# Moving short waits in TensorE's order: the decay check's transpose, the logits of blocks 1 to 3, the last second product, the steps beside row copies, and busy matmuls in the first block

## Chip, cores, metric

One core of one Trainium2 chip. The metric is device time of one execution in microseconds (us); the number quoted is the median of several executions, with lowest and highest where they matter. "Span" is the profiled time from the first to the last instruction, some 1.7 us shorter than the device time of the same execution. "Clock" is the mean clock granted to TensorE, 1.00 at full rate.

## The reference, cut to what matters

```python
def _attn_ref(q, k, v, f_logit):          # (4, 8, 768, 48), fp32
    f = 1.0 / (1.0 + np.exp(-f_logit))
    for t in range(S):
        state = f[:, :, t, :, None] * state + np.einsum('bhd,bhe->bhde', k[:, :, t], v[:, :, t])
        y[:, :, t] = np.einsum('bhd,bhde->bhe', q[:, :, t], state)

def _moe_ref(x, w_in, w_out):             # (3072, 384), (384, 2048), (2048, 384)
    h = x @ w_in
    sp = np.maximum(h, 0.0) + np.log1p(np.exp(-np.abs(h)))
    return (h * erf(sp)) @ w_out
```

Attention with a decaying state feeds a product to 2048 hidden columns, an activation, and a product back to 384 columns. All is fp32.

## The kernel before: the parts that matter here

The sequence is cut into 24 chunks of 128 rows; three chunks make a block, and there are 8 blocks. TensorE's order is written by hand. Iteration `it` has one slot per matmul of the hidden product of block `it` (48 slots, 12 per group) and, from `it` 2 on, of the second product of block `it - 2` (48 slots, between the hidden groups); from `it` 2 to 7, where both run, an iteration is called a mixed stage. The profile counts two passes for each of these matmuls (x96 for the 48 slots of a second product). VectorE's or ScalarE's copy of a finished hidden product out of PSUM is called its eviction. Between slots stand pieces of the attention of block `it + 1`, steps of the activation (`act_step`) and steps that round weights.

```python
def prepare(blk, j0, j1):                 # logits of a block: VectorE, then ScalarE twice
    ...
    nc.vector.tensor_scalar(out=lt, in0=lt, scalar1=LOGIT_MIN, scalar2=None, op0=ALU.max)
    ...
    nc.scalar.activation(out=lt, in_=lt, func=AF.Exp, scale=-1.0)
    nc.scalar.activation(out=lt, in_=lt, func=AF.Ln, bias=1.0)

def stage_d(g):                           # decay sums of chunk g
    ...
    nc.tensor.matmul(ps, lhsT=tri[:], rhs=lts[blk][:, j, :], start=True, stop=True)
    nc.scalar.activation(out=dp..., in_=ps..., func=AF.Exp, scale=-1.0)
    nc.scalar.activation(out=kd, in_=ps..., func=AF.Exp)
    nc.vector.tensor_tensor(out=qd..., in0=qns[...]..., in1=dp..., op=ALU.mult)
    ...
# stage_t(g): transposes of qd and kd, copied to SBUF as qT and kT by ScalarE
# stage_s(g): scores; VectorE makes A = scores * tri; state product dS; VectorE makes Sn
# stage_y(g): y = products of A with v and of the state with qT; copied to xT by ScalarE

def project(blk):                         # second product
    ops = [ps_moe.tile([P, 2, 512], FP32, name="ops", tag="moe") for _ in range(2)]
    ...                                   # row copies: osb2 <- ops[0], osb1 <- ops[1], on ScalarE

def check_decays():
    nc.vector.tensor_reduce(out=low[:], in_=Tall..., axis=AX.X, op=ALU.min)
    ps = ps_at.tile([P, 512], FP32, name="ps_f", tag="at")
    nc.tensor.transpose(ps[0:1, 0:P], low[:], ident[:])
    ...                                   # VectorE: minimum of the row, flag

def keep_busy(n):                         # matmuls whose result nobody reads
    ps = ps_sc.tile([P, 2, HP, P], FP32, name="busy", tag="sc")
    for _ in range(n):
        nc.tensor.matmul(ps[:, 0, 0, :], lhsT=tri[:], rhs=tri[:], start=True, stop=True)

for it in range(n_blocks + 2):            # cut
    for s, _ in enumerate(slots(it)):
        ...
        if step:
            act_step()
        if it + 2 < n_blocks and s == n // 2:
            prepare(it + 2, 0, CPB)
        if it == n_blocks - 1 and s == 5:
            check_decays()
```

## Time and profile before

| | before |
|---|---|
| time, median of 3 | 657.68 us (657.57 to 657.77) |
| profiled execution | 656.5 us, span 654.8 us |
| TensorE busy | 632.7 us, 97% of the span |
| mean clock | 0.990 |

The prediction shows the lines that carry the argument. Four more are fixed points of TensorE's order, from the timeline of the kernel before (start, duration, engine, line, operation, output and inputs, and in brackets the idle time before it with its releaser).

```profile
31.17 2.85 PE L480 MATMUL hps<-xT,w_in_sb 128*128 128x384 f32 x8 [0.64 <-ACT xT L421]
...
65.91 1.45 PE L480 MATMUL hps<-xT,w_in_sb 128*128 128x384 f32 x4
...
148.40 3.81 PE L480 MATMUL hps<-xT,w_in_sb 128*128 128x384 f32 x11 [0.33 <-DVE Hg L492]
...
198.99 1.56 PE L480 MATMUL hps<-xT,w_in_sb 128*128 128x384 f32 x4 [1.08 <-ACT osb L521]
```

These four are the first hidden product, the product after the first sum of block 2, the point where TensorE waits for VectorE's eviction, and the pause behind the second row copy of the first mixed stage.

### The profile page before, as it was taken

How to read it: one execution, taken by the hardware profiler on the slowest of the kernel's cores; microseconds unless marked ns; L12 is line 12 of the kernel's file. 1: busy time of each engine (PE TensorE's matmuls, PEld its weight loads, DVE VectorE, ACT ScalarE, POOL GpSimd, SP SyncE). 2: the span in 40 equal slices, each digit the busy share in tenths (PEclk: the TensorE clock that was granted, in tenths of full speed). 3: DMA queues.
4: the chain of work that ended last, by engine and by line, in shares of the span. 5: the costliest groups of instructions: out<-in, count | busy, mean ns of one | idle time of the engine just before them, and what ended most of it. 6: DMA issues, size and time to landing. Idle time of an engine off the chain costs nothing.

```text
span 654.8 us, 9308 instructions
## 1 busy us (share of the span) xinstructions
PE 632.7 (97%) x3785; PEld 393.2 (60%) x3785; DVE 475.7 (73%) x440; ACT 509.9 (78%) x459; POOL 69.2 (11%) x61
## 2 busy tenths in 40 slices
PE   8889998999999999999999999999999989999996
PEld 6756655665655666656666666666666555555553
DVE  4889897997778966778667877688676667587710
ACT  5355655679899988996897978997797969899800
POOL 0112101120110001301310002202020000000000
PEclk9899999999999999999999999999999989999999
DMA  9996952310104120221204201120000000000001
GB/s 195 252 264 156 295 120 37 74 25 14 37 25 85 25 37 13 61 49 25 37 13 98 36 13 24 38 49 1 2 0 37 1 0 1 36 0 2 36 2 40
DMA packets 120689, 36.90 MB, mean 56 GB/s; under 512 B 112448, under 2 KB 115520, under 8 KB 120640
## 3 DMA queue, kind: packets, MB, share of 16 engines
q1 hardware_dynamic: 118560, 35.84, 23.6%
q10 hardware_dynamic: 2080, 0.39, 0.4%
q8 instruction: 32, 0.52, 0.3%
q14 instruction: 17, 0.14, 0.1%
HBM read 31.46 MB, written 4.72 MB: 55 GB/s over the span
## 4 chain that ended last, share of the span: by engine, by line
PE 72%; ACT 12%; DVE 10%; issue 4%; POOL 0%; DMA 0%; SPq 0%; DVEq 0%; POOLq 0%; ACTq 0%
PE ops L509 30%; PE hps L480 29%; ACT x L153 5%; PE y L147 5%; DVE e L158 3%; PE sc L366 3%; PE ps_d L323 2%; PE ps_t L350 2%; ACT L446 1%; ACT yl L435 1%; ACT L297 1%; ACT e L446 1%; PE dS L394 1%; ACT e L431 1%; DVE w_out_sb L272 1%
## 5 line engine op out<-in xcount | busy, mean ns | idle before, releaser
L480 PE MATMUL hps<-xT,w_in_sb 128*128 128x384 f32 x768 | 262.7, 493 | 2.4 <-ACT osb L521 1.1
L509 PE MATMUL ops<-w_out_sb,Hg 128*128 128x384 f32 x768 | 256.1, 489 | 1.5 <-ACT osb L516 1.5
L158 DVE SCALAR_TENSOR_TENSOR e<-x,e 128x1536 f32<-128x1536 f32 x128 | 230.0, 1797 | 5.1
L153 ACT ACTIVATE x<-yl,serf_bias 128x1536 f32<-128x1536 f32 x128 | 195.3, 1566 | 15.2 <-DVE e L158 15.1
L509 PEld LDWEIGHTS ops<-w_out_sb,Hg 128*128 128x128 f32 x768 | 143.8, 190 | 99.7 <-ACT osb L516 2.1
L480 PEld LDWEIGHTS hps<-xT,w_in_sb 128*128 128x128 f32 x768 | 143.7, 192 | 99.7 <-issue 5.3
L449 DVE TENSOR_TENSOR Hg<-Hg,e 128x1536 f32<-128x1536 f32 x32 | 56.2, 1757 | 64.5 <-ACT e L446 64.4
L340 POOL TENSOR_TENSOR kd<-kn,kd 128x384 f32<-128x384 f32 x21 | 34.7, 1652 | 325.5 <-issue 186.3
L492 DVE COPY Hg<-hps 128x768 f32<-128x768 f32 x48 | 45.8, 954 | 20.4 <-PE hps L480 20.0
L446 ACT ACTIVATE e<-e 128x1536 f32<-128x1536 f32 x32 | 47.5, 1483 | 9.8 <-DVE e L158 9.6
L435 ACT ACTIVATE yl<-e 128x1536 f32<-128x1536 f32 x32 | 47.5, 1484 | 0.3
L431 ACT ACTIVATE e<-Hg 128x1536 f32<-128x1536 f32 x32 | 47.2, 1476 | 0.0
L336 DVE TENSOR_TENSOR qd<-qn,dp 128x384 f32<-128x384 f32 x24 | 15.8, 658 | 37.1 <-ACT dp L326 37.1
L410 POOL TENSOR_TENSOR Mbd<-Sn,Tall 48x192 f32<-48x192 f32 x32 | 33.3, 1041 | 88.1 <-DVE Sn L407 71.4
L297 ACT ACT_TABLE_LOAD x31 | 39.8, 1283 | 1.3 <-PEq L915 0.8
L446 ACT ACT_TABLE_LOAD x31 | 39.8, 1283 | 0.6
L147 PE MATMUL y<-A,vt 128*32 128x128 f32 x768 | 36.5, 283 | 1.0 <-DVE A L380 1.0
L147 PEld LDWEIGHTS y<-A,vt 128*32 128x32 f32 x768 | 28.1, 111 | 13.2 <-issue 6.1
L380 DVE TENSOR_TENSOR A<-sc,tri 128x1024 f32<-128x1024 f32 x24 | 29.3, 1220 | 8.5 <-PE sc L366 8.1
L147 PE MATMUL y<-qT,Mbd 128*32 128x128 f32 x480 | 31.2, 280 | 0.0
L366 PEld LDWEIGHTS sc<-qT,kT 48*128 48x128 f32 x384 | 23.3, 187 | 12.5 <-issue 10.6
L421 ACT COPY xT<-y 128x384 f32<-128x384 f32 x24 | 11.3, 472 | 24.0 <-PE y L147 24.0
(70 smaller groups left out, 384.9 us busy)
## 6 DMA issues: line engine op xcount, KB each, us to landing
lt<-in_f_logit_dram SPq DMA_DIRECT2D x24, 192.0 KB, 4.1
qn<-in_q_dram SPq DMA_DIRECT2D x24, 192.0 KB, 3.3
Hg<-in_moe_w_out_dram SPq DMA_DIRECT2D x6, 768.0 KB, 5.5
kn<-in_k_dram SPq DMA_DIRECT2D x23, 192.0 KB, 3.3
vt<-in_v_dram SPq DMA_DIRECT2D x23, 192.0 KB, 3.1
w_out_sb<-in_moe_w_in_dram SPq DMA_DIRECT2D x4, 768.0 KB, 6.4
Hg<-in_moe_w_in_dram SPq DMA_DIRECT2D x4, 768.0 KB, 7.8
out_dram<-osb SPq DMA_DIRECT2D x8, 384.0 KB, 2.5
```

The costliest lines, as they stand in the source:

```text
L147: nc.tensor.matmul(y[M * i : M * (i + 1), kt, :], lhsT=terms[n][0], rhs=terms[n][1], start=(n == 0), stop=(n == len(terms) - 1), skip_grou ...
L153: nc.scalar.activation(out=dst[:], in_=y[:], func=AF.Square, bias=serf_bias[:, i : i + 1], scale=SERF_K)
L158: nc.vector.scalar_tensor_tensor(out=e[:], in0=x[:], scalar=SERF_AB[i][1], in1=e[:], op0=ALU.add, op1=ALU.mult)
L297: nc.scalar.add_instruction(mybir.InstLoadActFuncSet(act_func_set_id=EXP_LN, name=nc.get_next_instruction_name(), engine=mybir.EngineType. ...
L366: nc.tensor.matmul(sc[:, r, a, :], lhsT=kT[rows(r), a, :], rhs=qT[rows(r), a, :], start=True, stop=True,)
L431: nc.scalar.activation(out=e[:], in_=h, func=AF.Exp)
L435: nc.scalar.activation(out=y[:], in_=e[:], func=AF.Ln, scale=SERF_C, bias=1.0)
L446: nc.scalar.activation(out=e[:], in_=e[:], func=AF.Tanh)
L449: nc.vector.tensor_tensor(out=h, in0=h, in1=e[:], op=ALU.mult)
L480: nc.tensor.matmul(hps[:, j, 0:TB], lhsT=w_in_sb[:, kt, ft * P : (ft + 1) * P], rhs=xTs[blk][:, kt, :], start=(kt == 0), stop=(kt == n_k - 1),
L492: nc.vector.tensor_copy(out=to, in_=hps[:, :, 0:TB])
L509: nc.tensor.matmul(ops[tt // 2][:, tt % 2, 0:d_model], lhsT=gr["h"][:, j, tt * P : (tt + 1) * P], rhs=w_out_sb[:, ft, :], start=(ft == 0), ...
```

## The change

The intent is to take pauses away from TensorE without adding useful work: issue what TensorE will wait for earlier (logits), or put the waiting instruction later (the check's transpose); keep ScalarE free where it has to copy rows; give the last product a PSUM tile that nobody has to empty; and cover the pauses of the first block with more matmuls that nobody reads, so that the clock stays up.

```diff
+    busy = []
+    def keep_busy(n):
+        for _ in range(n):
+            nc.tensor.matmul(busy[-1], lhsT=tri[:], rhs=tri[:], start=True, stop=True)
 # stage_d, block 0: the tile of the decay sums
+            busy.append(both[:, 1, P : 2 * P])
 # stage_t, after the transposes of qd
+            if 0 < g < CPB and src is qd:
+                keep_busy(3)
 # stage_y, before y
+        if blk == 0:
+            keep_busy(3)
 # project
-        ops = [ps_moe.tile(...) for _ in range(2)]
+        ops = [ps_moe.tile(...) for _ in range(2 if blk < n_blocks - 1 else 1)]
+        if blk == n_blocks - 1:
+            ops.insert(0, ps_sc.tile([P, 2, 512], FP32, name="ops", tag="sc"))
 # check_decays: a generator in two parts
         nc.vector.tensor_reduce(out=low[:], ..., op=ALU.min)
+        yield
         nc.tensor.transpose(ps[0:1, 0:P], low[:], ident[:])
         ...
+        yield
 # ahead of the first block
+        first = ps_sc.tile([P, 2, HP, P], FP32, name="busy", tag="sc")
+        busy.append(first[:, 0, 0, :])
 # first block
         stage_y(1)
+        prepare(1, 0, CPB)
         ...
         stage_y(2)
         ...
-        prepare(1, 0, CPB)
 # the loop over slots
-                if step:
+                if step and not 66 <= s < 72:
                     act_step()
-                if it + 2 < n_blocks and s == n // 2:
+                if it + 2 < n_blocks and s == (16 if it < 2 else n // 2):
                     prepare(it + 2, 0, CPB)
-                if it == n_blocks - 1 and s == 5:
-                    check_decays()
+                if it == n_blocks - 1 and s in (5, 40):
+                    next(check)
```

The old `keep_busy`, which wrote to a tile of its own, is removed. Its two calls at the start stay, but the second of them (behind the first sum) now writes to the tile of the decay sums as well. The skipped steps are two in the first mixed stage (slots 67 and 70) and one in each later one.

## The prediction

> **What bounds the kernel now.** I began with the page: busy time by engine, and the row of the granted clock.
>
> ```profile
> PE 632.7 (97%) x3785; PEld 393.2 (60%) x3785; DVE 475.7 (73%) x440; ACT 509.9 (78%) x459; POOL 69.2 (11%) x61
> ...
> PEclk9899999999999999999999999999999989999999
> ```
>
> TensorE has work in 97% of the span, so only three things shorten it: fewer matmuls, fewer pauses of TensorE, or fewer matmuls at a low clock. No useful matmul is removed, so I look for pauses and for low clock (the two 8s in the clock row). Next, the list of waits, for PE alone; columns are total us, times, longest.
>
> ```profile
> PE ps_d L323 <- ACT lt L312: 3.9, 4, 2.0
> PE ps_f L546 <- DVE low L542: 2.9, 1, 2.9
> PE ps_t L350 <- ACT qT L354: 1.7, 2, 1.0
> PE ops L509 <- ACT osb L516: 1.5, 1, 1.5
> ...
> PE hps L480 <- ACT osb L521: 1.1, 1, 1.1
> ...
> PE y L147 <- DVE A L380: 1.0, 1, 1.0
> ```
>
> All PE waits of that list sum to some 16 us; the diff names nearly every line of it. Then stretches of 4 us; after PE, PEld, DVE, ACT and POOL busy comes the granted clock, the third number from the right. Of all such stretches before the tail, only these have a clock under 1.00.
>
> ```profile
> 24.00:28.00 4.00, 3.02 (x56) 2.79 (x55) 2.92 (x7) 0.34 (x1) 0.48 (x1) 0.87 0.86 165
> 28.00:32.00 4.00, 3.36 (x51) 2.65 (x44) 3.90 (x5) 1.30 (x2) 1.12 (x2) 0.70 1.02 269
> 112.00:116.00 4.00, 3.67 (x6) 2.06 (x7) 1.47 (x3) 3.05 (x5) 0.98 (x1) 0.57 0.01 0
> 524.00:528.00 4.00, 2.27 (x5) 1.36 (x6) 2.10 (x4) 3.31 (x3) 0.00 (x0) 0.66 0.00 0
> 528.00:532.00 4.00, 4.00 (x13) 2.37 (x12) 0.62 (x1) 3.43 (x3) 0.00 (x0) 0.91 0.00 0
> ```
>
> So a pause is paid twice where it lets the clock fall. The timeline shows the pauses one by one (start, duration, and in brackets the idle time and its releaser):
>
> ```profile
> 112.33 1.65 PE L323 MATMUL ps_d<-lt,tri 128*128 128x384 f32 x2 [2.04 <-ACT lt L312]
> 114.53 0.56 DVE L336 TENSOR_TENSOR qd<-qn,dp 128x384 f32<-128x384 f32 x1 [3.19 <-ACT dp L326]
> ...
> 525.73 0.37 PE L546 MATMUL ps_f<-ident,low 128*1 128x128 f32 x1 [2.88 <-DVE low L542]
> ...
> 617.95 31.23 PE L509 MATMUL ops<-w_out_sb,Hg 128*128 128x384 f32 x96 [1.47 <-ACT osb L516]
> ...
> 623.41 1.76 DVE L449 TENSOR_TENSOR Hg<-Hg,e 128x1536 f32<-128x1536 f32 x1 [1.55 <-ACT e L446]
> ```
>
> TensorE stands still at 110.3 for the logits of block 3, at 522.9 for the decay check's minimum, and at 616.5 for a copy of output rows that frees PSUM.
>
> **What the Trainium skill says.** (1) "TensorE: Matmul & The Clock Gate", Part 1: the array's clock has two states, half and full; activity is watched in free-running windows of about 3.4 us, and an idle window brings half rate. The trace agrees on the two states (0.50 in each us from 27 to 30), but not that only an idle window does it: pauses of 0.98, 2.04 and 2.88 us were enough here, in stretches with many short matmuls. (2) The same page, Part 2, step 1: TensorE alone reorders, and only weight loads; matmuls keep program order, and the other engines' queues are in order. The trace agrees: all later matmuls stood 2.88 us behind one 128x128 transpose. So moving an instruction in the order can be worth its whole wait. (3) "PSUM — Partial Sum Buffer", Specifications: 8 banks per partition. The kernel's pools take them all (2 scores, 2 attention, 4 second stage), so another buffer for the last product must be borrowed. (4) "ScalarE: Activation LUTs", What ACT_TABLE_LOAD costs: some 1283 ns per load; the trace's mean is 1283 ns.
>
> **The change part by part.**
>
> *Decay check.* The minimum stays where it was; its transpose comes 35 slots of TensorE later. In the order as built it has no semaphore left to wait for. Removed: 2.88 us, and the low clock after it: four weight loads at 526.54, 527.18, 527.82 and 528.46 are 0.64 us apart where 0.32 is usual, 4 x 0.32 = 1.3. VectorE, which empties the PSUM tile, is idle 4.78 us there, so it takes no part of this. **-4.2 us.**
>
> *Logits of block 3* (the prepare of slot 24 moved to slot 16; eight slots at some 0.65 us, with attention work between them, put it over 5 us earlier). Removed: 2.04 us and the low clock: 1.65 instead of some 0.9 for the sum, 3.07 instead of 2.1 for six passes, together 1.7. So 3.7 us of TensorE. But VectorE works almost without a pause from 114.5 to 159.5, and TensorE waits for it again at 148.4 (0.33 us, for an eviction). VectorE gains only its own pause, 3.19 less some 0.3. The rest becomes a longer wait at 148.4. **-2.9 us.** *Blocks 1 and 2*: the same wait is 0.71 us at 34.73 and 0.48 at 65.16. **-1.2 us.**
>
> *No activation steps where rows are copied.* In the first mixed stage the two row copies stood at 192.07 and 198.48, with squares between; TensorE paused 0.39 and 1.08 us. As built they now stand side by side. ScalarE is full there, so the first pause stays. **-1.1 us.** In later stages such copies cost TensorE nothing.
>
> *Last second product in the scores' PSUM.* It starts without the copy at 617.12. **-1.5 us.**
>
> *Busy matmuls.* Six groups of three are new, 18 x 2 passes x some 0.116 us (from 12 passes in 1.50 at full clock) = 0.7 us per group. Three lie in pauses of 1.01, 0.68 and 0.98 us and cost nothing; two lie where TensorE did not pause (before the y of chunks 0 and 1), one in the pause before y of chunk 2 with part of the pause left. And a dependency is new: they write to the tile of the decay sums, and as built the first group after each sum waits for ScalarE's second exponential of that tile. For chunk 0 the exponential ends at 7.95, where busy matmuls ran from 6.88: later copies queue behind other ScalarE work anyway, so of 1.1 us about 0.2 remain. For chunk 2 it ends at 17.47, where y began at 16.50: with 0.7 of busy work y begins 1.9 later. By the chunk-1 y the delay is 2.5; then the pauses of 0.98 us and behind A take up part, and y of chunk 2 begins at some 29.7 instead of 27.33. If the clock stays full it takes 1.7 instead of 3.2, and the first hidden product starts 0.9 later than 31.17; if it still falls, 2.0 later. I take the middle: **+1.4 us.**
>
> *What is given back in the tail.* Skipping one step in each mixed stage puts the activation work further behind. Counting the steps slot by slot, and in the built order, one whole group more remains behind the row copies of block 5: 12.83 us of ScalarE (distance of its table loads, 568.31 to 581.58 to 594.41 to 607.24). Before, the last tanh ended 55.9 us after the copy at 567.50; now 55.9 + 12.8 + 1.8 (it waits for the second copy) = 70.5, and the product on VectorE ends at 72.3. TensorE needs it after 112 slots of 0.645 us = 72.3. A tie: **+0.3 us.**
>
> Sum: -4.2 - 2.9 - 1.2 - 1.1 - 1.5 + 1.4 + 0.3 = -9.2, so 657.7 - 9.2 = **648.5 us**, 1.4% less.
>
> **Rivals.** (A) *The new waits at the start weigh more*: the busy groups stall TensorE at every exponential and the clock falls all the same, because a busy group is short against the window. For it: the waits are in the built order, and before the change 0.98 us of pause was enough. Against: after 31 us weight rounding has over 4 us in hand. Time: 650 to 651. (B) *ScalarE becomes the bound of the tail*: the tie above falls on the wrong side by a step or two, or VectorE takes all of the gain at 148.4. For it: ScalarE is full from 568 to 620. Time: 651 to 653. (C) *Nothing is given back*: the start costs nothing and the clock stays full throughout; -4.2 -3.7 -1.2 -1.5 -1.5 and -1.4 from the start: 644 to 645. Against: VectorE's full stretch. (D) *The pause at 522.9 was hidden*, so its removal only moves it. Against: TensorE runs from there to 616 with no pause over 0.3 us.
>
> **Range and chances.** The two large terms (4.2 and 2.9) rest on pauses that the trace shows directly; the start may be off by 1.5, the tail by 2, the VectorE stretch by 1. Together about 3 either way, a little more upward: 645 to 652. Two per cent faster needs 644.5, the best of (C): 0.06. Slower by 2% has no mechanism: 0.01. Within 2%: 0.93.
>
> **What would show it.** Right: no PE wait for `ps_f`; none of 0.4 us or more for the logits; PE clock 1.00 around 112 and 524; a longer PE wait for VectorE's eviction near 145; the last product following the one before it with no pause, and ScalarE's last tanh within 2 us of the slot that needs it. The first hidden product starts at 32 to 33. Wrong: a first hidden product before 31 or after 34; a clock under 1.00 in the first 35 us together with a start later than 33; a pause over 2 us inside the last product; or a new pause in the stages from 200 to 500, where I expect none.

## The result, and the profile after

| | before | after |
|---|---|---|
| time, median of 4 each | 657.62 us (656.17 to 657.77) | 648.09 us (648.01 to 648.13) |
| profiled span | 654.8 us | 646.4 us |
| TensorE busy | 632.7 us | 630.7 us |
| mean clock | 0.990 | 0.998 |

The ratio is 0.986, with a 95% interval of 0.984 to 0.988. A ratio here is the mean time of one kernel's fast runs over that of the other's in the same rounds, so it is not quite the ratio of the medians quoted.

First the page of the kernel after: TensorE's busy time and the row of the clock, in which the two 8s are gone.

```profile
PE 630.7 (98%) x3815; PEld 393.8 (61%) x3815; DVE 474.6 (73%) x440; ACT 510.0 (79%) x459; POOL 59.1 (9%) x61
...
PEclk9999999999999999999999999999999999999999
```

Then the list of TensorE's waits of the kernel after (total us, times, longest):

```profile
PE ps_t L357 <- DVE Sn L416: 2.5, 2, 1.6
PE ps_d L320 <- ACT kd L336: 1.9, 2, 1.0
...
PE ops L524 <- DVE Hg L460: 1.2, 1, 1.2
...
PE hps L491 <- ACT osb L531: 0.4, 1, 0.4
```

The waits for `low`, for the logits `lt` and for the copy ahead of the last product are no longer in it. Of the lines shown, the first is new and was not predicted, the second was, and the third only as a tie. Most of the stretches that had a low clock before, of the kernel after (columns as in the prediction; the clock is the third number from the right):

```profile
28.00:32.00 4.00, 3.46 (x82) 2.96 (x81) 3.53 (x6) 1.44 (x2) 1.61 (x2) 1.00 0.99 239
...
112.00:116.00 4.00, 4.00 (x40) 2.66 (x39) 3.86 (x4) 2.55 (x4) 1.81 (x1) 1.00 0.08 4
...
524.00:528.00 4.00, 4.00 (x14) 2.41 (x13) 4.00 (x4) 4.00 (x4) 0.00 (x0) 1.00 0.00 0
528.00:532.00 4.00, 4.00 (x14) 2.33 (x13) 3.08 (x4) 3.98 (x3) 0.00 (x0) 1.00 0.00 0
```

All are at 1.00, and 24 to 28 is too. Last, the timeline of TensorE of the kernel after, at the fixed points and at the new waits:

```profile
7.76 1.60 PE L320 MATMUL ps_d<-tri 128*128 128x128 f32 x12 [0.96 <-ACT kd L336]
...
17.45 0.94 PE L320 MATMUL ps_d<-tri 128*128 128x128 f32 x6 [0.96 <-ACT kd L336]
...
32.19 2.85 PE L491 MATMUL hps<-xT,w_in_sb 128*128 128x384 f32 x8 [0.61 <-ACT xT L432]
...
37.36 0.63 PE L357 MATMUL ps_t<-ident,qd 128*128 128x128 f32 x4 [0.40 <-DVE qd L343]
...
60.26 0.63 PE L357 MATMUL ps_t<-ident,kd 128*128 128x128 f32 x4 [1.59 <-DVE Sn L416]
...
66.48 1.45 PE L491 MATMUL hps<-xT,w_in_sb 128*128 128x384 f32 x4
...
118.57 0.63 PE L357 MATMUL ps_t<-ident,kd 128*128 128x128 f32 x4 [0.90 <-DVE Sn L416]
...
146.01 4.14 PE L491 MATMUL hps<-xT,w_in_sb 128*128 128x384 f32 x12 [0.33 <-DVE Hg L503]
...
577.31 54.34 PE L524 MATMUL ops<-w_out_sb,Hg 128*128 128x384 f32 x168
632.90 8.01 PE L524 MATMUL ops<-w_out_sb,Hg 128*128 128x384 f32 x24 [1.25 <-DVE Hg L460]
```

The difference of the two kernels at each fixed point is a ledger. Each row's change is the difference at this point less that at the row above. The last column is the same change with the second profile of the kernel before (`before_again`, below) in the place of the first.

| up to | before, us | after, us | change in the row | predicted | against `before_again` |
|---|---|---|---|---|---|
| first hidden product | 31.17 | 32.19 | +1.0 | +1.4 | +1.8 |
| product behind the transposes of block 1's first chunk | 39.03 | 38.62 | -1.4 | -0.7 | -2.9 |
| product behind the first sum of block 2 | 65.91 | 66.48 | +1.0 | -0.5 | +0.6 |
| product behind VectorE's eviction | 148.40 | 146.01 | -3.0 | -2.9 | -1.5 |
| y behind the row copies of the first mixed stage | 200.48 | 196.74 | -1.3 | -1.1 | -1.4 |
| first second product of the stage with the check | 538.92 | 530.76 | -4.4 | -4.2 | -4.6 |
| end of the last matmul | 649.18 | 640.91 | -0.1 | -1.2 | -0.1 |

The sum is -8.3 us; the spans differ by 8.4. The last column sums to -8.1: the total is steady, but its split over the first four rows moves by up to 1.5 us with where the low clock fell in one execution. Two rows are off by more than 1 us: block 2 and the end. The two 54.34 and 8.01 us runs of the last two products show the end: no pause where the last product begins, but one of 1.25 us for the last activated group, 8 us before the end.

The wait at 60.26 was not predicted. ScalarE's timeline shows how it comes about; before:

```profile
52.36 0.80 ACT L490 COPY Hg<-hps 128x768 f32<-128x768 f32 x1
53.65 0.49 ACT L326 ACTIVATE dp<-ps_d 128x384 f32<-128x384 f32 x1 [0.49 <-PE ps_d L323]
```

and after:

```profile
52.02 1.16 ACT L311 ACTIVATE lt<-lt 128x1152 f32<-128x1152 f32 x1 [0.19 <-DVE lt L307]
53.22 1.16 ACT L312 ACTIVATE lt<-lt 128x1152 f32<-128x1152 f32 x1
54.29 0.78 ACT L501 COPY Hg<-hps 128x768 f32<-128x768 f32 x1
54.97 0.49 ACT L333 ACTIVATE dp<-ps_d 128x384 f32<-128x384 f32 x1
```

The logits of block 2, at slot 16 now, stand ahead of an eviction and of the exponentials of chunk 5, which come 1.3 us later; VectorE's `qd`, `A` and `Sn` follow 1.3 us later in turn (`A` at 58.24 instead of 56.92), and the transposes of `kd` wait for them: their PSUM tile is the one from which `Sn` is made.

### The profile page after: what moved, and what is told of

Its sections match the earlier page's. It is cut to its first block, busy times and chain, and to the rows that moved or that the text cites. A ratio compares the mean times of both kernels' runs of the same rounds, so it can differ in the third digit from the quotient of the medians.

```text
span 646.4 us, 9360 instructions
## 1 busy us (share of the span) xinstructions
PE 630.7 (98%) x3815; PEld 393.8 (61%) x3815; DVE 474.6 (73%) x440; ACT 510.0 (79%) x459; POOL 59.1 (9%) x61
## 4 chain that ended last, share of the span: by engine, by line
PE 75%; ACT 12%; DVE 8%; issue 3%; DMA 1%; POOL 0%; DVEq 0%; POOLq 0%; ACTq 0%
PE hps L491 32%; PE ops L524 27%; PE y L147 5%; ACT x L153 5%; PE sc L375 4%; DVE e L158 3%; PE ps_t L357 3%; PE ps_d L330 2%; ACT yl L446 1%; ACT e L457 1%; PE dS L403 1%; ACT L297 1%; ACT e L442 1%; ACT L457 1%; DVE Hg L460 1%
## 5 line engine op out<-in xcount | busy, mean ns | idle before, releaser
L491 PE MATMUL hps<-xT,w_in_sb 128*128 128x384 f32 x768 | 259.9, 490 | 1.3 <-ACT xT L432 0.6
L347 POOL TENSOR_TENSOR kd<-kn,kd 128x384 f32<-128x384 f32 x21 | 29.4, 1401 | 323.1 <-issue 185.7
L343 DVE TENSOR_TENSOR qd<-qn,dp 128x384 f32<-128x384 f32 x24 | 14.2, 591 | 36.6 <-ACT dp L333 36.6
L297 ACT ACT_TABLE_LOAD x31 | 39.8, 1283 | 1.3 <-PEq L929 0.8
L457 ACT ACT_TABLE_LOAD x31 | 39.8, 1283 | 0.5
L419 POOL TENSOR_TENSOR Mbd<-Sn,Tall 48x192 f32<-48x192 f32 x32 | 28.6, 893 | 97.0 <-DVE Sn L416 82.3
L147 PE MATMUL y<-A,vt 128*32 128x128 f32 x768 | 35.2, 277 | 0.1
```

Source lines behind the costliest of these rows:

```text
L147: nc.tensor.matmul(y[M * i : M * (i + 1), kt, :], lhsT=terms[n][0], rhs=terms[n][1], start=(n == 0), stop=(n == len(terms) - 1), skip_grou ...
L297: nc.scalar.add_instruction(mybir.InstLoadActFuncSet(act_func_set_id=EXP_LN, name=nc.get_next_instruction_name(), engine=mybir.EngineType. ...
L457: nc.scalar.activation(out=e[:], in_=e[:], func=AF.Tanh)
L491: nc.tensor.matmul(hps[:, j, 0:TB], lhsT=w_in_sb[:, kt, ft * P : (ft + 1) * P], rhs=xTs[blk][:, kt, :], start=(kt == 0), stop=(kt == n_k - 1),
```

## The experiments

All but the last are the kernel after with one edit (two in the filled version and the first combination, three in the second). They ran on three chips, four kernels on each, beside the kernel before, whose medians there were 656.27, 656.48 and 656.8 us. The kernel after itself was timed only in its own session, at 648.09, where the kernel before stood at 657.62. The traces show that the chips can be compared all the same: at the product behind VectorE's eviction, ahead of where their edits act, `check_back`, its filled version, `steps_back`, `steps_first_stage` and `last_product_back` stand at 145.95 to 146.17, the kernel after at 146.01. Differences below some 0.3 us are not read. All runs gave correct results.

**The check's transpose back behind its minimum** (first chip).

```diff
-                if it == n_blocks - 1 and s in (5, 40):
+                if it == n_blocks - 1 and s == 5:
+                    next(check)
                     next(check)
```

> The changed kernel (648.1 us) with the decay check's transpose put back right behind its minimum. Theory: the pause of some 2.9 us returns (VectorE's minimum ends 2.9 us after TensorE gets there in the changed kernel's trace, too) and the clock falls for some 2.7 us after it, 4.3 together: 652.4 us, with a stretch of clock 0.6 to 0.7. Rival (the pause was hidden behind ScalarE's full tail, which sets the end in the changed kernel): 648 to 649.

Measured: 653.12 us (651.36 to 654.32), 5.0 more than after. The stretches of its profiled execution (654.32 us):

```profile
520.00:524.00 4.00, 1.79 (x4) 1.17 (x5) 2.58 (x5) 3.29 (x4) 0.00 (x0) 0.67 0.00 0
524.00:528.00 4.00, 4.00 (x7) 1.99 (x6) 0.00 (x0) 3.91 (x3) 0.00 (x0) 0.50 0.00 0
```

The wait of 2.9 us is back, and so is a low clock, here for all of 4 us. The fastest of the four runs lost only 3.3 us, little more than the wait, the slowest 6.2.

**The same, with 12 matmuls that nobody reads ahead of the transpose** (first chip).

```diff
+        for _ in range(12):
+            nc.tensor.matmul(ps[:, P : 2 * P], lhsT=tri[:], rhs=tri[:], start=True, stop=True)
         nc.tensor.transpose(ps[0:1, 0:P], low[:], ident[:])
```

> The same, with 12 busy matmuls of 128x128 ahead of the transpose (2.8 us at full clock), which keep the array at work while it waits. Theory (two separate costs, the wait and the low clock): the wait stays, the clock holds at 1.00, so 2.9 us more than the changed kernel, 651.0 us. Rival (the clock falls for a reason other than the array's idleness, or costs nothing by itself): as without them, 652.4.

Measured: 651.14 us (651.01 to 651.30); the wait for `low` is 0.20 us and the clock is 1.00 from 520 to 528. The pause is filled, not saved, so its 3.0 us are still lost; the clock's part (2.0 us of the median) is gone, and with it the spread: 0.3 us instead of 3.0. The check's term therefore has two parts: a wait of 2.9 us that is always paid, and a low clock that cost from 0.4 to 3.3 us in these four runs (their time above the kernel after, less 2.9).

**Without the new busy matmuls** (first chip).

```diff
-            if 0 < g < CPB and src is qd:
-                keep_busy(3)
-        if blk == 0:
-            keep_busy(3)
```

> The changed kernel without its six new groups of busy matmuls. Theory (the groups and their waits for ScalarE cost the start 1.0 us more than the full clock gives back): first hidden product at 31.2 instead of 32.2, clock near 0.5 around 27 to 30, 647.1 us. Rival (the low clock is the dearer of the two, and lasts or returns): first hidden product at 32.5 or later, 649 us or more.

Measured: 650.64 us, with runs of 648.55, 648.80, 652.48 and 653.56. The expectation was wrong in sign: no run was faster than the kernel after. In the profiled (slowest) run the clock stood at half from 28 us on:

```profile
28.00:32.00 4.00, 3.22 (x56) 2.79 (x56) 3.83 (x7) 0.54 (x2) 1.61 (x2) 0.50 1.09 288
32.00:36.00 4.00, 3.56 (x6) 2.05 (x7) 3.52 (x5) 1.21 (x2) 0.00 (x0) 0.50 1.15 281
...
64.00:68.00 4.00, 3.92 (x36) 2.42 (x40) 3.86 (x6) 0.59 (x1) 0.83 (x2) 0.64 0.91 243
```

The first hidden product began at 32.45 us and its eight passes took 5.49 us instead of 2.85. So the busy groups cost 1.0 us of start in the ledger, and what they buy is not a shorter start but a steady one: 0.1 us of spread instead of 5.0.

The run does not isolate the clock. Without the groups TensorE gets earlier to chunk 2, and VectorE's first step on the logits of block 1, which the change moved ahead of that chunk's `A`, has to wait for their transfer:

```profile
25.30 0.76 DVE L307 TENSOR_SCALAR lt<-lt 128x1152 f32<-128x1152 f32 x1 [0.97 <-DMA lt<-in_f_logit_dram]
```

So the pause ahead of y of chunk 2 was 1.77 us here, against 0.98 in the kernel before, and the low clock began in it. How much of the 5.0 us of spread is the clock alone was not tested. (One of the two waits of 0.96 us stays in this run, at 8.32: it belongs to the old second call.)

**The activation steps back** (first chip), and later **only the first mixed stage without them** (second chip).

```diff
-                if step and not 66 <= s < 72:
+                if step:                                      # steps_back
+                if step and not (it == 2 and 66 <= s < 72):   # steps_first_stage
```

> The changed kernel with activation steps allowed again where rows are copied. Theory (two opposite effects): the second pause of the first mixed stage returns, 1.1 to 1.4 us, and the wait of 1.25 us inside the last product goes, as ScalarE has one group less left in the tail: 648.0 to 648.3 us, and no wait for the eviction product near 633. Rival (the skipped steps are a plain gain): 649.3 or more. Rival (they only harm): 647 or less.

> The changed kernel with the steps skipped in the first mixed stage alone, where the copies made TensorE wait. Theory (the skips of the later stages only put a group into the tail): no wait of 1.25 us inside the last product and no pause at 196, 646.8 us. Rival (the later skips matter too): 648.1 or more.

Measured: 647.97 us with all steps back, 646.78 us (646.66 to 646.95) with only the first stage's left out. With all back, a pause of 1.08 us behind the second row copy is there again and the last products run through; the two cancel. With only the first stage's left out, the gain stays and the tail's wait is gone too, as its timeline shows: 192 passes in one run.

```profile
577.34 62.08 PE L524 MATMUL ops<-w_out_sb,Hg 128*128 128x384 f32 x192
```

This is the fastest version that I measured, 1.3 us below the kernel after. That the tail's wait comes from the steps left out in later stages is shown by these two runs.

**The logits of block 2, then of block 3, back to the middle of their iteration** (second chip).

```diff
-                if it + 2 < n_blocks and s == (16 if it < 2 else n // 2):
+                if it + 2 < n_blocks and s == (16 if it == 1 else n // 2):   # logits2_back
+                if it + 2 < n_blocks and s == (16 if it == 0 else n // 2):   # logits3_back
```

> The changed kernel with the logits of block 2 alone back at slot 24. In its trace their earlier place makes ScalarE late for chunk 5's exponentials, and a new TensorE wait of 1.59 us stands at 60.26 where 0.48 us was saved. Theory (this part costs what it was to save, and the delay is carried on): 647.1 us, with the 1.59 us wait gone and one of 0.5 for the logits back. Rival (VectorE's full stretch up to 146 takes up the difference): 648.1.

> The changed kernel with the logits of block 3 alone back at slot 24. Theory (TensorE's pause of 2.0 us returns, in some runs with low clock behind it, but only VectorE's share of it reaches the rest): 650.3 us where the clock holds, up to 651.2 where it falls. Rival (the whole of 3.7 us counts): 651.8. Rival (VectorE's full stretch hid it): 648.1.

Measured: 647.17 us (646.97 to 647.28) and 650.45 us (650.41 to 651.20). Moving the logits of block 2 early costs 0.9 us; moving those of block 3 early gains 2.4. With block 2's back, the 1.59 us wait is gone and the old one of 0.47 returns. With block 3's back, the pause of 2.04 us returns with a clock of 0.77 from 112 to 116. That low clock does not show in the time: the profiled run, at a mean clock of 0.996, took 650.41 us, two at 0.999 took 650.41 and 650.50, and the slowest, 651.20, had 1.000. In the trace it begins only at 114.18, behind the sum for which VectorE waits.

**The last second product back in the second stage's PSUM** (second chip).

```diff
-               for _ in range(2 if blk < n_blocks - 1 else 1)]
-        if blk == n_blocks - 1:
-            ops.insert(0, ps_sc.tile([P, 2, 512], FP32, name="ops", tag="sc"))
+               for _ in range(2)]
```

> The changed kernel with the last second product back in its own two buffers. Theory (in the changed kernel ScalarE's last group, not this buffer, sets the end): the product starts some 1.9 us later, behind the row copy, but the wait of 1.25 us inside it goes, so only 0.6 us more: 648.7 us. Rival (the part is worth its pause): 649.6 to 650.0.

Measured: 649.00 us (648.73 to 649.28), 0.9 more than after. A pause of 1.83 us for the row copy stands at 610.23 and the wait for the last group is gone: TensorE comes later and finds it done. The part is worth less than its pause because ScalarE's last group sets the end behind it.

**Six busy matmuls ahead of y of chunk 2 only** (third chip, 5 rounds).

```diff
-        if blk == 0:
-            keep_busy(3)
+        if g == CPB - 1:
+            keep_busy(6)
```

> The changed kernel with busy matmuls only where TensorE pauses anyway: none before the y of chunks 0 and 1, six instead of three before the y of chunk 2. Theory (the groups in the pauses keep the clock, the others only delay): first hidden product at 30.2 to 30.6, clock 1.00, 646.4 us with a spread of 0.3. Rival (the groups outside of the pauses are needed too, as the whole start is near the limit): low clock in some runs, 647 to 651, spread over 1 us.

Measured: 647.87 us, with runs from 646.61 to 653.22; both numbers of the expectation were wrong. The first hidden product did start 1.5 us earlier, at 30.67. It was worth nothing at 60 us: there the wait for `Sn` grew from 1.59 to 3.18 us, and ended at nearly the same time as before. VectorE's timeline names what holds it:

```profile
51.01 0.76 DVE L307 TENSOR_SCALAR lt<-lt 128x1152 f32<-128x1152 f32 x1 [1.51 <-DMA lt<-in_f_logit_dram]
...
55.27 0.56 DVE L343 TENSOR_TENSOR qd<-qn,dp 128x384 f32<-128x384 f32 x1 [1.86 <-ACT dp L333]
```

The logits of block 2 arrive at 51 us, and at slot 16 everything of chunk 5 stands behind them. And two of the six runs had a low clock somewhere: 650.65 us at a mean of 0.995 and 653.22 at 0.990. Fewer busy groups, less steady.

**Two combinations** (third chip): the first has the steps of the first stage only and the logits of block 2 at slot 20; the second has the six busy matmuls as well.

```diff
-                if step and not 66 <= s < 72:
+                if step and not (it == 2 and 66 <= s < 72):
-                if it + 2 < n_blocks and s == (16 if it < 2 else n // 2):
+                if it + 2 < n_blocks and s == (20, 16)[it] if it < 2 else it + 2 < n_blocks and s == n // 2:
```

> The changed kernel with steps skipped in the first mixed stage alone, and the logits of block 2 at slot 20. Theory (the two gains add, and slot 20 spares both the old wait of 0.5 and the new one of 1.6): 646.8 minus 1.0 minus 0.5 to 0.8, so 645.1 us. Rival (another group or VectorE's full stretch takes up the second gain): 646.2 or more.

> Both edits together with the busy matmuls in the pauses. Theory (all three add): 643.4 us. Rival (the start gains nothing or the clock falls): 645 or more, with a spread over 1 us.

Measured: 649.95 us (649.54 to 650.18) and 650.71 us (649.06 to 653.41). Both were meant to be the best version and are slower than the kernel after. Against the first stage's steps alone, slot 20 costs 3.2 us in the first (649.95 less 646.78), so it is worse than slot 16 and than the middle. ScalarE's timeline of the first, and TensorE's wait:

```profile
59.56 1.16 ACT L311 ACTIVATE lt<-lt 128x1152 f32<-128x1152 f32 x1 [3.73 <-DVE lt L307]
60.76 1.16 ACT L312 ACTIVATE lt<-lt 128x1152 f32<-128x1152 f32 x1
...
63.29 0.59 ACT L363 COPY qT<-ps_t 128x512 f32<-128x512 f32 x1
```

```profile
63.93 0.43 PE L147 MATMUL y<-A,vt 128*32 128x128 f32 x8 [3.13 <-ACT qT L363]
```

At slot 20 the logits no longer stand ahead of chunk 5's exponentials, but ahead of its copy of `qT`, for which y of chunk 4 has to wait too (the two transposes' tiles and y share one PSUM pool of two). ScalarE itself stood still for 3.73 us ahead of them: VectorE's step on the logits, at 58.76, had come to stand behind `A` and `Sn` of chunk 4. The pause of 3.13 us took the clock down to 0.59 from 64 to 68. In both the tail's wait was gone, as with the first stage's steps alone. The second adds nothing but unsteadiness: its profile has the wait for `qT` too, one of 1.7 us more for VectorE ahead of the six matmuls (VectorE waited 2.10 us for the transfer of block 1's logits), and its runs spread over 4.4 us.

**The kernel before once more** (third chip, one look).

> The kernel before once more, for a second look at its clock. Theory (the pauses at 27, 110 and 523 fall now and then into a low clock, by chance): pauses of the same length as in the first trace, but at least one of the three low-clock stretches of another length or missing. Rival (the low clock belongs to the pause): the same three stretches.

Measured: 656.23 us, clock 0.995. Two of its stretches, to be held against those in the prediction:

```profile
28.00:32.00 4.00, 3.38 (x61) 2.56 (x62) 3.83 (x6) 1.31 (x2) 1.61 (x2) 1.00 1.02 287
112.00:116.00 4.00, 2.60 (x8) 1.44 (x8) 1.54 (x3) 3.75 (x6) 0.64 (x1) 1.00 0.00 0
```

The large pauses are the same in place and size (2.88, 2.04 and 1.50 us), but the clock stayed at 1.00 at 28 and at 112, and fell only behind the check (0.69 and 0.88 from 524 to 532). One pause differs: the first hidden product began at 30.38, 0.8 us earlier than in the first profile, and the logits of block 1 came no earlier.

```profile
35.41 0.91 PE L323 MATMUL ps_d<-lt,tri 128*128 128x384 f32 x2 [2.18 <-ACT lt L312]
```

One profile's low clock is one draw. Over the three chips, 25 runs of the kernel before, timed beside the other experiments, went from 654.57 to 661.04 us; the four of the kernel after stayed within 0.12 us.

## Why the prediction was right, and where not

The time is 0.4 us from the predicted one. Part of that is luck: the ledger of the two profiles sums to -8.3 rather than -9.2, and the runs that made the 657.68 were 1.2 us longer than the profiled one. Held against the medians of the kernel before on the three chips (656.27 to 656.8), 648.09 is a gain of 8.2 to 8.7 us.

- **The decay check**, -4.2, was right (ledger -4.4, undone it costs 5.0). Its split into wait and low clock is shown by the filled version. The low clock's part is not a constant; the end of this section tells what it goes with.
- **The logits of block 3**, -2.9, were right in size (-3.0; undone 2.4), but this too is in part the draw: against `before_again`, where the clock held and a VectorE instruction behind the sum took 1.77 us instead of 2.56, it is -1.5. One detail of the way was wrong: what VectorE could not give did not show as a longer wait at the eviction, which stayed at 0.33 us, but as a new one of 0.90 us at 118.57, for its state sums `Sn`.
- **The logits of block 1** were under-rated: -1.4 up to the second product instead of -0.7. Besides the wait for the logits, the 1.01 us wait for `kd` at 38.54 became one of 0.40 for `qd`. This row and the start are one balance: where the clock holds at the start, TensorE only waits longer for the logits (2.18 us in `before_again`). No run undid this part alone.
- **The logits of block 2** are the step that failed. The sentence "the same wait is 0.71 us at 34.73 and 0.48 at 65.16", with -0.5 booked for the second, counted the wait removed and not what the two activations (2.4 us on ScalarE) are put in front of. The ledger has +1.0, and undoing the move gains 0.9. I read the order on TensorE and did not read it on ScalarE at that slot. The same unread order made both combinations fail at slot 20.
- **The start**: +1.4 booked, as the middle of +0.9 (full clock) and +2.0; +1.0 found, and the clock stayed full, as hoped. The prediction miscounted: five groups of three are new, not six (3815 passes instead of 3785, so 15 matmuls of two passes); it counted the pause of 0.98 us twice. The two waits of 0.96 us behind ScalarE's second exponential stand where they were predicted, at 7.76 and 17.45. But the term is not a price without return: without the new groups the runs lose from 0.5 to 5.5 us, the wait for block 1's logits included.
- **The row copies**: -1.1 booked, -1.3 found; the first pause stayed at 0.39 us.
- **The last product and the tail**: -1.5 and +0.3 booked, -1.47 and +1.25 found. The mechanism was right, ScalarE's last tanh comes nearly as late as the counting says: it was to end 70.5 us after the copy of block 5's rows and ended 71.6 after it (559.45 to 631.05). The microsecond between is a term that the sum left out. The two row copies of block 6 now fall into the last group but one, which they lengthen: its table load and the next stand 13.89 us apart, not 12.83.

```profile
601.03 1.28 ACT L297 ACT_TABLE_LOAD   x1
...
614.92 1.28 ACT L297 ACT_TABLE_LOAD   x1
```

Before, these copies fell into the last group, where ScalarE had to wait for VectorE anyway; from the end of one tanh to that of the next, the last group takes 10.56 us in both kernels. The product on VectorE was to end 72.3 us after the copy, when TensorE would need it, and ended after 73.4. A tie was called, and one microsecond decided it. (The prediction also speaks of one step skipped in each mixed stage; in the first it is two.)

- **Rivals.** (A) did not come true, since the clock held; the experiments with fewer groups show only that it does fall there in some runs. (B) came true for about 1 us of its three. (C) fell at the start (+1.0, not -1.4), at block 2 and in the tail. (D) fell: nothing took the check's place from 200 to 577.

**What goes with the low clock.** The traces, read again us by us after the experiments, show more than the text above used. Seven of the fourteen have low clock ahead of the end, in eleven stretches. Each lasts a whole multiple of 3.41 us: nine last 3.4, one 6.8 (`check_back`), one 10.2 (`no_new_busy`). Within a trace they begin a whole number of such windows apart: in the first profile at 26.96, 112.30 and 525.32, which is 25 and 121 windows. So in these traces the clock changes window by window, on a grid that stays fixed within an execution. It goes with how much TensorE worked within one window, more than with how long a pause is:

| trace and pause | window | TensorE busy in it, us | clock in the window behind it |
|---|---|---|---|
| `before`, 2.04 at 110.29 | 108.88 to 112.30 | 1.40 | 0.50 |
| `before_again`, 2.04 at 111.36 | 109.11 to 112.53 | 2.25 | 1.00 |
| the same pause's second half | 112.53 to 115.94 | 2.54 | 1.00 |
| `before`, 2.88 at 522.85 | 521.90 to 525.32 | 0.95 | 0.50 |
| `combined`, 3.13 at 60.80 | 61.33 to 64.74 | 0.81 | 0.50 |
| `check_back`, 1.60 at 58.65 | 57.15 to 60.57 | 1.82 | 1.00 |

In `before_again` the pause of 2.04 us lay across a line of the grid, so neither window lost enough. In nine of the eleven cases TensorE was busy for 0.54 to 1.75 us of the window ahead of the first low one. The other two are at the start (2.80 us busy from 23.55 in `before`, 2.67 from 24.16 in `no_new_busy`), so busy time alone does not decide there. Full rate came back behind every low window in which TensorE was busy for 3.00 us or more (eleven), and not behind those with 2.40, 2.57 and 2.78. This reading was made after the fact and no run tested it.

What stays open: what brings the low clock at the start, where the window was busy for over 2.6 us; many of the matmuls there are of 48 rows or of one column, but no run varied that. The prediction's "in stretches with many short matmuls" fits only there: the windows ahead of the low ones at 112 and 525 hold five and three passes. And whether the first stage's steps alone with the logits of block 2 in the middle would add up to some 645.9 us (646.78 less 0.9, an estimate); this was not run.

## What to carry to other kernels

When an instruction is moved forward, read the order of every engine it touches: what stands behind it there may be what the next wait is for, and a gain of 0.5 us on one engine can be a loss of 1.0 through another. A pause of TensorE has two prices. One is its length, or less where another engine sets the end: all 2.9 us at the check, but 0.9 of 1.83 ahead of the last product. The other is the clock, here in whole windows of 3.4 us at half rate, with chance in where the pause falls; the matmuls that nobody reads took away only this second one at the check, and showed in the spread as much as in the median. When work is put off to keep an engine free, follow it to the end of the program: only the stage where the pause was had something to gain, the later ones paid 1.3 us at the tail.

## What the Trainium skill lacked or had wrong

- "TensorE: Matmul & The Clock Gate", Part 1, ties the half rate to an idle window of about 3.4 us, on a window that runs freely. The length and the grid agree with the traces (3.4, 6.8 and 10.2 us). It gives no figure for how little work is too little. Here the windows ahead of half rate were not idle, but busy for 0.54 to 1.75 us, and 2.67 and 2.80 at the start; a pause of 2.04 us was enough in one execution (0.57 from 112 to 116 us) and not in another (1.00). Nor does it give one for how busy a window must be to bring full rate back: here 3.00 us and more did, 2.40, 2.57 and 2.78 did not.
- "ScalarE: Activation LUTs", What ACT_TABLE_LOAD costs, adds a drain of about 1380 ns to each load. Here the load takes 1283 ns and the next activation follows with no such gap: in the kernel after, a load from 601.03 for 1.28 us, an activation at 602.32, and the activation ahead of it (599.54, for 1.47) ends 0.02 us before the load.
- No page that I read tells the cost of a busy matmul that shares its PSUM tile with a value still being read: here it was 0.96 us, twice, for a tile written in another part than the one read. The wait is in the program as built; no run shows whether the chip needs it.
